# A retention layer with a SwiGLU feed-forward on one core: one pair's preparation and the end transposes earlier in the written order, and 29 stores issued by GpSimd

## The chip, the cores and the metric

The kernel runs on one core of a Trainium2 chip. The metric is the device time of one execution in microseconds; lower is better. A core has TensorE (PE; PEld is its loading of weights), VectorE (DVE), ScalarE (ACT), GpSimd (POOL) and SyncE (SP, which only issues transfers here). They run on their own and meet at semaphores. Transfers can be issued by SP, ACT and POOL; all of them are carried out by the same 16 DMA engines.

## The reference

```python
# q, k, v: 8 x 8 heads x 576 x 64, float32
scores = q @ k.transpose(0, 1, 3, 2) / sqrt(64)
gamma = 1 - 2 ** (-5 - arange(8))                  # one per head
Dmat = where(i >= j, gamma ** (i - j), 0)          # i: query, j: key
attn = (scores * Dmat) @ v                         # no softmax
x = attn.transpose(0, 2, 1, 3).reshape(4608, 512)
g = x @ w_gate                                     # 512 x 1536, float64 as given
out = (g * sigmoid(g) * (x @ w_val)) @ w_out       # 1536 x 512; out is 4608 x 512, float32
```

## The kernel before, in words

The attention is done in chunks of 64 tokens, for 32 pairs of heads (8 batches, 4 pairs each). Because the decay is a power of gamma, each chunk needs only its own scores, and a 64 x 64 state that carries all earlier chunks. The work on a pair is a pipeline of `tick(t)`: pair t is prepared (`transposes`: ScalarE multiplies the keys by powers of gamma at line 531, VectorE transposes q and k at line 516), pair t-1 gets its states (TensorE, line 567) and scores (line 597), and pair t-2 gets its values (lines 556, 583), which go to the matrix x. The first four pairs leave out their last chunk. These four last chunks are done together: GpSimd loads them early (`end_loads`, lines 711 and 716), VectorE transposes them (`end_transposes`, line 721), and TensorE makes their scores at line 727 (`end_scores`), as part of tick 6.

The weights are given as 64-bit floats. They are loaded in 18 blocks (lines 394 and 396), each block in two halves, and each half is turned to 32-bit: `split(j)` on ScalarE (lines 413, 414) takes the bits apart, and `rounding(j)` on VectorE (lines 430, 431) puts them together again. `rounding(j)` also writes `split(j + 1)` into ScalarE's order. A block's place in SBUF is reused, so a split also releases the load of a later block.

The feed-forward is done in tiles of tokens. The first tile (512 tokens) uses the weights as they are: `up0(f)` for 12 groups of features (TensorE into two of four PSUM banks, ScalarE's Silu at line 880, VectorE's product at line 881), then `down0(f)` (line 888). The later four tiles of 1024 tokens replace 32 block products by 26: the tables `UP`, `DOWN` and `OUT_SUMS` say which sums of blocks are multiplied. The sums of weights are made once. Those of w_gate and w_val are made by GpSimd during the first large tile (`w_sums`, through `add` at line 910, and line 1078) and sent to DRAM. Those of w_out are made earlier, during the first tile, for each third (`qd`) of the 1536 rows: GpSimd makes thirds 0 and 1, VectorE third 2 (`out_sums`, through `add`, lines 903 to 910). Each third has 26 sums of 128 x 256, made in 9 groups; a sum goes into a free place (six for GpSimd at first, six more from the last up0 on), is stored in DRAM by a transfer at line 961 that SP issues, and its place is free when that transfer has landed and no later sum reads it. A few of the 26 are a block itself, and need no sum.

The order is written out by hand: the schedule is manual, and each engine does its instructions in the order in which the program emits them. The list `plan` (lines 1217 to 1247) emits the roundings, `up0`, the ticks, the loads of later pairs and the first ten groups of sums. After it comes the loop over `down0` with the rest of the groups. SP's queue is in order too: it holds loads of q, k and v (lines 306, 311) and the stores of line 961, and a transfer whose condition isn't met holds those behind it.

Of the kernel before, what the change touches and what calls it, by code (L numbers as in the profile page):

```python
# [155 lines left out]
def kernel(  # L156
# [32 lines left out]
    nc = tc.nc  # L189
# [5 lines left out]
    HP = H // 2  # L195
# [7 lines left out]
    TB = TW // 4  # L203
# [63 lines left out]
    def whole(i):  # L267

        return HP <= i < needed(2) - 2
# [194 lines left out]
    def light(i):  # L464

        return needed(1) - 6 <= i < needed(2) - 2
# [119 lines left out]
    def scores(i, alone):  # L586

        qT = st[i]["qT"]
        for hl in range(0 if i < HP else 2):
            at = ts(NC - 1, L)  # L590
            nc.tensor.matmul(sr[half[hl]], kT[half[hl], at], qT[half[hl], at],  # L591
                             start=alone, stop=True, skip_group_check=True)
        for c in range(NFULL):
            for hl in range(2):
                for r in range(2):
                    at = ts(2 * c + r, L)
                    nc.tensor.matmul(sc[chunk(i, hl, 2 * c + r)[0], r if whole(i) else hl, c], kT[half[hl], at], qT[half[hl], at],  # L597
                                     start=True, stop=True, skip_group_check=True)
# [162 lines left out]
    def tick(t, lo=HP, hi=NP, spread=False, then=None):  # L761
        go_on(len(pieces))
        if hi == HP:

            def new_pair():
                scores(t - 1, True)
                new_states(t - 1)
                pieces.extend(masked(t - 1))
                go_on(3)

            scale_run(t + 1)
            if lo < t < hi:
                new_pair()
            if lo <= t - 2 < hi:
                own_values(t - 2)
            for f in transposes(t) if lo <= t < hi and t + 1 < HP else ():
                f()
            if lo <= t - 2 < hi:
                earlier_values(t - 2)
                if t == HP:  # L780
                    up0(0, range(2))
                to_x(t - 2)[0]()
            if t + 1 == HP:
                split(0)
                after = transposes(t)
                rounding(0)
                for f in after:
                    f()
            if t == HP:
                rounding(2)  # L790
                rounding(3, False)
                new_pair()
                while held:
                    held.pop()()
                split(4)
                up0(1, range(2))
            return
        if lo <= t - 2 < hi:
            own_values(t - 2)
            if t == HP + 3:  # L800
                st[t - 2]["own"] = end_own(1)
        if lo <= t - 1 < hi:
            new_states(t - 1)
        if lo <= t - 2 < hi:
            earlier_values(t - 2)
            if t == HP + 3:
                end_own(0)
                end_earlier()
        if lo <= t - 1 < hi:
            scores(t - 1, t - 2 < lo)  # L810
            if t == HP + 2:
                end_scores()
        if lo <= t - 1 < hi and whole(t - 2) and not whole(t - 1):
            decay(slice(0, H), slice(0, H), half[1])
        copies, *masks = masked(t - 1) if lo <= t - 1 < hi else (lambda: None,)
        keys, *new = transposes(t) if lo <= t < hi else (lambda: None,)
        outputs = to_x(t - 2)[0] if lo <= t - 2 < hi else lambda: None
        late = needed(1) - 4 <= t < needed(1) - 2 or light(t - 2)
        if late and masks:
            own, (last, pairs, odd, evens) = masks  # L820
            pieces.extend([lambda: (copies(), own(), last(), outputs()), [pairs, odd, lambda: (evens(), keys())]])
        elif late:
            pieces.append(lambda: (copies(), outputs(), keys()))
        else:
            pieces.extend([lambda: (copies(), keys()), outputs])
            for own, (last, pairs, *rest_of) in [masks] if masks else []:
                pieces.extend([own, [lambda: (last(), pairs()), *rest_of]])
        if then and new:
            pieces.extend(new[:-1])
            pieces.append(lambda: (new[-1](), then()))  # L830
        else:
            pieces.extend(new)
            pieces.extend([then] if then else [])
        if t == HP + 2:
            pieces.append(end_masks)
        if t == HP + 3:
            pieces.append(end_to_x)
        if not spread:
            go_on(len(pieces))
# [8 lines left out]
    def go_on(n):  # L848
        for _ in range(min(n, len(pieces))):
            while part_on():  # L850
                pass
# [61 lines left out]
    dn_ops = [dr.tile([P, 768], F32, name=f"dn{i}") for i in range(N)]  # L913
# [5 lines left out]
    x0_places = [rest[:, x0_at + TB * i : x0_at + TB * (i + 1)] for i in range(8)]  # L919
    vector_places = x0_places + more_places[6:] + [rest[:, part_at + TB * i : part_at + TB * (i + 1)] for i in range(8)]  # L920

    events = []
    for line in OUT_SUMS:
        i, s = line.split("|")
        slot, ops = s.split(":")
        events += [(int(op[1]), op) for op in terms(ops)] + [(None, int(slot), int(i))]

    def out_sums(qd):


        place = {}

        def free(p):
            if not any(p is q for q in x0_places):
                sum_places.append(p)

        eng, sum_places = (nc.vector, vector_places) if qd + 1 == NQ else (nc.gpsimd, pool_places)

        def view(s):
            return w_dn[:, qd, s // 2, s % 2] if s < 8 else place[s]  # L940

        def used(e):
            return [e[1]] if e[0] is None else [int(a) for a in e[1][2:]]

        def release(k):

            for s in list(place):
                for e in events[k + 1 :]:
                    if s in used(e):
                        break  # L950
                    if s == e[0]:
                        free(place.pop(s))
                        break
                else:
                    free(place.pop(s))

        def do(k):
            e = events[k]
            if e[0] is None:
                _, slot, i = e  # L960
                nc.sync.dma_start(out=dn_ops[i][:, qd * TB : (qd + 1) * TB], in_=view(slot))
            else:
                new = sum_places.pop(0)
                add(eng, e[1], view, new)
                if e[0] in place:
                    free(place[e[0]])
                place[e[0]] = new
            release(k)

        r, ends = [], [k for k, e in enumerate(events) if e[0] is None]  # L970
        for g in range(0, N, 3):
            lo, hi = ends[g - 1] + 1 if g else 0, ends[min(g + 2, N - 1)] + 1

            def group(lo=lo, hi=hi):
                for k in range(lo, hi):
                    do(k)

            r.append(group)
        return r
# [228 lines left out]
    FIRST = needed(1) - 2  # L1208
# [8 lines left out]
    plan = []  # L1217

    def round_until(i):
        while todo and order.index(i) >= todo[0]:  # L1220
            m = todo.pop(0)
            plan.extend(lambda j=j: rounding(j) for j in (2 * m, 2 * m + 1))

    round_until(3)
    tick_at = {2: 4, 3: 5, 5: 6, 7: 7, 10: 8, 11: 9}
    for f in range(2, NF):
        round_until({4: 12, 6: 13, 8: 14, 9: 15, 10: 16, 11: 17}.get(f, f + 2))
        if f == 2:
            plan.append(lambda: tick(HP, HP, FIRST))
        plan.append(lambda f=f: up0(f, range(HP)))  # L1230
        if f - 1 in tick_at and f < 7:
            plan.append(lambda t=tick_at[f - 1]: next_load(t))
        if f in tick_at and f > 2:
            if tick_at[f] == HP + 2:
                plan.append(end_transposes)
            plan.append(lambda t=tick_at[f]: tick(t, HP, FIRST))
        if f in (7, 10, 11):
            plan.append(lambda t=tick_at[f]: next_load(t))
        for _ in range({7: 3, 10: 4, 11: 3}.get(f, 0)):
            if f >= (7, 10, NF)[groups[0][0]]:  # L1240
                if f + 1 == NF and more_places:
                    plan.append(lambda places=more_places[:6]: pool_places.extend(places))
                    more_places.clear()
                plan.append(lambda group=groups.pop(0)[1]: group())
    assert not todo
    for f in plan:
        f()
    tick_at = {1: 10, 3: 11, 6: 12, 8: 13}
    for m, f in enumerate(down_order):
        down0(f)  # L1250
# [77 lines left out]
```

## Time and profile before

| | us |
|---|---|
| median of 3 runs (lowest, highest) | 1043.01 (1038.88, 1045.0) |
| the profiled execution | 1040.52 |
| its span, first to last instruction | 1038.8 |
| TensorE busy in it | 1022.6 |
| VectorE busy | 634.5 |
| GpSimd busy | 428.7 |
| ScalarE busy | 298.3 |

The page of a profile gives the busy time of each engine, then the span in 40 slices of 26 us: each digit is the busy share of a slice in tenths. Further views give the waits (engine, line, what it waited for: total us, times, longest), and the timeline (start in us, duration in us, engine, line, operation, tiles written <- read, shapes, count; in brackets the idle time before it and what ended that). "SPq" and "ACTq" are transfers being issued. A line in the profile can be that of a helper: line 910 is an addition from `add`, whoever called it.

### The profile page before, as it was taken

To read this page: it belongs to the slowest core of one execution; us is meant where nothing else is said; L and a number is where in the kernel's file an instruction comes from. 1 tells how busy PE (TensorE), PEld (TensorE's weight loads), DVE (VectorE), ACT (ScalarE), POOL (GpSimd) and SP (SyncE) were. 2 spreads that over 40 slices of the span, in tenths; PEclk is the share of its full clock that TensorE was granted. 3 is DMA by queue.
4 is the path that set the end of the run, shared out by engine and by line. 5 is a ranking of instruction groups with operands and counts; after the bars stand their busy time and mean duration, and the time that the engine had idled before them with its cause. 6 is when DMAs were issued, how large, how long until landed. Compare 5 with 4: busy or idle time off the path is not lost.

```text
span 1038.8 us, 21564 instructions
## 1 busy us (share of the span) xinstructions
PE 1022.6 (98%) x8440; PEld 846.2 (81%) x8440; DVE 634.5 (61%) x1070; ACT 298.3 (29%) x649; POOL 428.7 (41%) x377
## 2 busy tenths in 40 slices
PE   6999999999999999999999999999999999999998
PEld 5644555888888888888888888888888888888887
DVE  5388878776758767546457685435466644344644
ACT  4375523243534222222322103223211022231110
POOL 3402367776575236622134058212242583222425
PEclk9999999999999999999999999999999999999999
DMA  9999877776779887674686687545554465555553
GB/s 245 249 279 257 198 208 268 210 206 192 192 201 245 227 249 217 179 198 140 187 223 178 177 201 218 152 138 153 154 174 149 145 197 150 155 153 161 180 163 100
DMA packets 307244, 199.12 MB, mean 192 GB/s; under 512 B 215944, under 2 KB 251784, under 8 KB 307144
## 3 DMA queue, kind: packets, MB, share of 16 engines
q1 hardware_dynamic: 275720, 161.17, 57.9%
q10 hardware_dynamic: 30784, 36.18, 10.5%
q8 instruction: 67, 1.10, 0.5%
q0 software_dynamic: 640, 0.39, 0.2%
q14 instruction: 33, 0.27, 0.1%
HBM read 157.58 MB, written 40.11 MB: 190 GB/s over the span
## 4 chain that ended last, share of the span: by engine, by line
PE 73%; DVE 0%; POOL 0%; ACT 0%; ACTq 0%; issue 0%; DVEq 0%
PE bankC L1107 11%; PE bankE L1107 11%; PE bankB L1107 11%; PE bankA L1107 11%; PE bankC L1156 7%; PE bankB L1156 7%; PE bankE L1156 7%; PE bankA L1156 7%; PE outer L556 1%; PE outer L583 1%; PE inner L597 1%; PE inner L567 1%; PE outer L591 0%; PE outer L579 0%; DVE arena L1134 0%; POOL arena L1078 0%
## 5 line engine op out<-in xcount | busy, mean ns | idle before, releaser
L1044 POOL TENSOR_TENSOR rest<-rest 128x512 f32<-128x512 f32 x65 | 91.6, 1414 | 234.7 <-DVE rest L1044 213.7
L1128 ACT ACTIVATE io<-rest 128x256 f32<-128x256 f32 x180 | 75.0, 416 | 302.5 <-DVE rest L1044 260.2
L1107 PE MATMUL bankC<-rest,arena 128*128 128x256 f32 x544 | 129.2, 381 | 0.0
L1107 PE MATMUL bankA<-rest,arena 128*128 128x256 f32 x544 | 128.8, 380 | 0.0
L910 POOL TENSOR_TENSOR arena<-arena 128x512 f32<-128x512 f32 (+1 forms) x72 | 110.8, 1551 | 35.8 <-DMA up<-arena 20.3
L1107 PE MATMUL bankE<-rest,arena 128*128 128x256 f32 x512 | 121.4, 380 | 1.0 <-DVE rest L1044 1.0
L1107 PE MATMUL bankB<-rest,arena 128*128 128x256 f32 x512 | 121.3, 380 | 0.2 <-DVE rest L1044 0.2
L1135 POOL TENSOR_TENSOR arena<-rest,io 128x256 f32<-128x256 f32 x72 | 51.9, 726 | 167.8 <-ACT io L1128 167.8
L1107 PEld LDWEIGHTS bankA<-rest,arena 128*128 128x128 f32 x544 | 103.3, 190 | 14.5 <-issue 0.7
L1107 PEld LDWEIGHTS bankC<-rest,arena 128*128 128x128 f32 x544 | 103.0, 190 | 14.4 <-POOL arena L910 0.3
L1107 PEld LDWEIGHTS bankE<-rest,arena 128*128 128x128 f32 x512 | 97.1, 190 | 14.5 <-DVE rest L1044 1.4
L1107 PEld LDWEIGHTS bankB<-rest,arena 128*128 128x128 f32 x512 | 97.2, 190 | 13.6 <-issue 0.6
L910 POOL TENSOR_TENSOR rest<-rest 128x256 f32<-128x256 f32 (+1 forms) x66 | 67.7, 1046 | 77.3 <-DVE rest L431 38.4
L1044 DVE TENSOR_TENSOR rest<-bankB,rest 128x512 f32<-128x512 f32 x72 | 48.9, 687 | 66.0 <-PE bankB L1107 51.7
L1044 DVE TENSOR_TENSOR rest<-bankC,rest 128x512 f32<-128x512 f32 x72 | 48.9, 688 | 65.7 <-PE bankC L1107 44.0
L1044 DVE TENSOR_TENSOR rest<-bankA,rest 128x512 f32<-128x512 f32 x72 | 48.9, 687 | 60.6 <-PE bankA L1107 44.1
L1044 DVE TENSOR_TENSOR rest<-bankE,rest 128x512 f32<-128x512 f32 x71 | 48.2, 688 | 59.6 <-PE bankE L1107 46.7
L1131 DVE SCALAR_TENSOR_TENSOR arena<-rest,io 128x256 f32<-128x256 f32 x84 | 58.6, 698 | 10.9 <-ACT io L1128 10.9
L1156 PE MATMUL bankB<-arena 128*128 128x256 f32 x252 | 58.2, 381 | 0.0
L1156 PE MATMUL bankC<-arena 128*128 128x256 f32 x252 | 58.2, 381 | 0.0
L1156 PE MATMUL bankE<-arena 128*128 128x256 f32 x252 | 57.9, 380 | 0.0
L1156 PE MATMUL bankA<-arena 128*128 128x256 f32 x252 | 57.9, 380 | 0.0
(205 smaller groups left out, 1632.3 us busy)
## 6 DMA issues: line engine op xcount, KB each, us to landing
arena<-up SPq DMA_DIRECT2D x234, 256.0 KB, 2.7
arena<-dn SPq DMA_DIRECT2D x104, 384.0 KB, 3.9
up<-arena ACTq DMA_DIRECT2D x78, 256.0 KB, 4.1
dn<-rest SPq DMA_DIRECT2D x78, 128.0 KB, 1.8
out_dram<-rest SPq DMA_DIRECT2D x31, 256.0 KB, 3.9
qk<-in_q_dram SPq DMA_DIRECT2D x108, 72.0 KB, 2.6
qk<-in_k_dram SPq DMA_DIRECT2D x108, 72.0 KB, 3.0
rest<-in_moe_w_out_dram ACTq DMA_DIRECT2D x6, 1024.0 KB, 5.7
```

Source lines behind the costliest of these rows:

```text
L556: m = nc.tensor.matmul(value(i, hl, c), s["v"][rows, at], ret[rows, c % 2 if whole(i) else hl, c // 2], start=start, stop=start, skip_grou ...
L567: nc.tensor.matmul(z[half[hl], r, c], s["kn"][chunk(i, hl, 2 * c + r)], s["v"][rows, at], start=True, stop=True, skip_group_check=True)
L583: nc.tensor.matmul(xr[half[hl]] if c + 1 == NC else value(i, hl, c), state[half[hl], c, :], s["qT"][half[hl], ts(c, L)], start=False, stop ...
L597: nc.tensor.matmul(sc[chunk(i, hl, 2 * c + r)[0], r if whole(i) else hl, c], kT[half[hl], at], qT[half[hl], at], start=True, stop=True, sk ...
L910: eng.tensor_tensor(out=dst, in0=srcs[0], in1=srcs[1], op=ALU.add if op[0] == "add" else ALU.subtract)
L1044: eng.tensor_tensor(out=at(op[1]), in0=at(op[2]), in1=at(op[3]), op=ALU.add if op[0] == "add" else ALU.subtract)
L1107: m = nc.tensor.matmul(b[:, gv * TB : (gv + 1) * TB], w[:, gv, ts(c, P)], rhs[:, c, :], start=(opens and gv == 0 and c == 0), stop=(c == 1 ...
L1128: nc.scalar.activation(out=s, in_=src[:, 0:TB], func=AF.Silu, scale=-1.0 if negative else 1.0)
L1131: return lambda: nc.vector.scalar_tensor_tensor(out=dst, in0=src[:, TB : 2 * TB], scalar=-1.0, in1=s, op0=ALU.mult, op1=ALU.mult)
L1135: nc.gpsimd.tensor_tensor(out=dst, in0=src[:, TB : 2 * TB], in1=s, op=ALU.mult)
L1156: nc.tensor.matmul(b[:, m * TB : (m + 1) * TB], lhs[:, qd, ts(m, P)], w[:, qd], start=(opens and qd == 0 and m == 0), stop=(qd == NQ - 1), ...
```

## The change

Three edits. The preparation of pair 4 (`tick(HP, HP, FIRST)`, which is only `transposes(4)`) was emitted after four roundings, just before `up0(2)`; now it is emitted after the first of them. The end transposes were emitted before tick 6; now they are emitted after tick 5. And a store of a sum that GpSimd made is issued by GpSimd itself as long as the plan is being emitted: these are the 26 stores of third 0 and the first three of third 1. The order of TensorE's instructions is the same as before; so is the order of the loads in SP's and ScalarE's queues.

```diff
+    down_begun = []
...
             if e[0] is None:
                 _, slot, i = e
-                nc.sync.dma_start(out=dn_ops[i][:, qd * TB : (qd + 1) * TB], in_=view(slot))
+                queue = nc.gpsimd if eng is nc.gpsimd and not down_begun else nc.sync
+                queue.dma_start(out=dn_ops[i][:, qd * TB : (qd + 1) * TB], in_=view(slot))
...
     round_until(3)
+    plan.insert(1, lambda: tick(HP, HP, FIRST))
     tick_at = {2: 4, 3: 5, 5: 6, 7: 7, 10: 8, 11: 9}
     for f in range(2, NF):
         round_until({4: 12, 6: 13, 8: 14, 9: 15, 10: 16, 11: 17}.get(f, f + 2))
-        if f == 2:
-            plan.append(lambda: tick(HP, HP, FIRST))
         plan.append(lambda f=f: up0(f, range(HP)))
...
         if f in tick_at and f > 2:
-            if tick_at[f] == HP + 2:
+            plan.append(lambda t=tick_at[f]: tick(t, HP, FIRST))
+            if tick_at[f] == HP + 1:
                 plan.append(end_transposes)
-            plan.append(lambda t=tick_at[f]: tick(t, HP, FIRST))
...
     for f in plan:
         f()
+    down_begun.append(True)
```

## The prediction

> **What bounds the kernel now.** I read the page first: the share of each engine, then the slices.
>
> ```profile
> PE 1022.6 (98%) x8440; PEld 846.2 (81%) x8440; DVE 634.5 (61%) x1070; ACT 298.3 (29%) x649; POOL 428.7 (41%) x377
> DMA  9999877776779887674686687545554465555553
> ```
>
> TensorE is busy for 98% of the span, so 1038.8 - 1022.6 = 16.2 us of waits is all that an edit of order can win. The DMA engines are full in the first four slices (to 104 us), which matters for anything that is stored earlier. Next, what TensorE waits for between 50 and 200 us, the stretch that the diff touches:
>
> ```profile
> PE inner L567 <- ACT kn L531: 1.2, 1, 1.2
> PE outer L727 <- DVE rest L721: 1.2, 1, 1.2
> PE bankE L1107 <- DVE rest L1044: 1.0, 1, 1.0
> PE bankB L1107 <- DVE rest L1044: 0.2, 1, 0.2
> ```
>
> Four waits, 3.6 us in all; outside them TensorE runs without a gap. The timeline places the first two:
>
> ```profile
> 50.91 0.66 ACT L413 ACTIVATE rest<-rest 128x512 f32<-128x512 f32 x1 [9.58 <-DMA rest<-in_moe_w_gate_dram]
> 54.85 0.96 ACT L531 ACTIVATE kn<-kn,tab 128x256 f32<-128x256 f32 x2
> 55.41 1.08 PE L567 MATMUL inner<-v,kn 64*64 64x64 f32 x29 [1.20 <-ACT kn L531]
> 73.65 0.76 DVE L721 STREAM_TRANSPOSE rest<-rest 128x256 f32<-128x256 f32 x2
> 74.47 0.46 PE L727 MATMUL outer<-rest 64*64 64x64 f32 x16 [1.16 <-DVE rest L721]
> ```
>
> ScalarE stood idle for 9.58 us until a weight block landed, and then did three splits before the keys of pair 4 (L531). VectorE reached the end transposes (L721) only after the product of up0(5). The third view is the queues and GpSimd:
>
> ```profile
> 119.18 6.11 POOL L910 TENSOR_TENSOR rest<-rest 128x256 f32<-128x256 f32 x7 [28.55 <-DMA dn<-rest]
> 137.59 0.72 POOL L910 TENSOR_TENSOR rest<-rest 128x256 f32<-128x256 f32 x1 [9.30 <-DMA dn<-rest]
> 168.34 3.38 POOL L910 TENSOR_TENSOR arena<-arena 128x512 f32<-128x512 f32 x2
> ```
>
> ```profile
> 114.22 9.41 SPq L961 DMA_DIRECT2D dn<-rest x9
> 123.73 3.42 SPq L306 DMA_DIRECT2D qk<-in_q_dram x4
> 131.35 45.42 SPq L961 DMA_DIRECT2D dn<-rest x69
> ```
>
> GpSimd has six places for sums. Their stores stand in SP's queue behind the loads of q, k and v, so GpSimd waits 28.6 and then 9.3 us, does its last 36 instructions for w_out from 137.6 to 168.3 us, and goes straight into the sums of the up weights, which TensorE reads from 176.3 us on. That it waited cost TensorE nothing there; what it does is to put GpSimd's sums beside VectorE's sums of x, and the last stores (176.3 us) ahead of them (VectorE waits 2.3 us for stores). The two waits of 1.27 us at 188 and 192 us are VectorE being late from this.
>
> **What the Trainium skill says.** "DMA: Bandwidth & Descriptors", section "Issuing engines are not separate DMA queues": the issuing engine saves only issue time, the transfers share 16 engines. This fits the full DMA row above. "SBUF — State Buffer", section "Who interferes with whom": a VectorE instruction with two SBUF inputs, or in a two-port mode, excludes GpSimd's reads and the other way round, while matrices read from PSUM don't. The trace agrees: a rounding (L430 and L431) takes 0.42 + 0.69 us alone, 0.94 + 1.10 at 120.6 us beside a sum; L604, which reads PSUM, keeps 0.69. The same page warns that software-made descriptors starve beside VectorE's two-port modes. The trace shows little of it: the twenty loads that GpSimd issued at 30 to 46 us took 548 to 763 ns each (128 pieces, as many as a store has), and the roundings beside them kept 0.42 and 0.69 us.
>
> **The change part by part.** TensorE's order is the same; SP loses 29 stores (26 of the first third of w_out, 3 of the second), GpSimd gains them; VectorE and ScalarE each have a group moved.
>
> *Keys and transposes of pair 4* now stand after one rounding instead of after four. Their k was issued at 38.7 us; loads near there took 7.1 to 7.9 us, so it is there at about 46.5, and the q and k for the transposes at 45.6. VectorE waits there (it idled from 43.4 to 51.6 us anyway); the transposes (0.77 + 0.74 us) end at 47.1 and the rounding behind them at 48.2, before TensorE needs it at 50.6. The keys (0.96 us) end at about 47.5, inside ScalarE's 9.58 us of idleness. Gain 1.20 us. What is late next is bank A: ScalarE read it at 55.70, after the keys; without them that is 54.85 to 55.45, and TensorE wants it at 57.05 - 1.20 = 55.85. It just fits.
>
> *The end transposes* move ahead of the roundings at 64.4 us. Their loads (issued to 46 us, 4.0 to 6.8 us to landing) are there. They cost VectorE 0.76 us, and the transposes and the product before them come earlier by about as much. Gain 1.16 us. So TensorE is ahead by 2.36 us at 75 us.
>
> *The stores on GpSimd.* Each costs it some 0.6 us of issue (548 to 763 ns above). The first third is 27 instructions at 0.855 us (30.8 us for the 36 above) and 26 stores: 23.1 + 15.6 = 38.7 us from about 83 us, to 122. The second is 23.1 + 3 x 0.6, to 147 us if nothing holds it. Before, it was 168.3. So there are 168.3 - 147 = 21 us of room, 0.8 us a store, for landings. About four places are in flight; if each store takes 6 to 7 us to land while the DMA engines are full (the small ones took 4.0 to 6.8 there), the pace is about 1.9 us a store and the first third ends near 132, the whole near 157. SP's load of pair 10, at 123.7 us behind nine stores, comes some 3 us sooner, and 29 x 0.4 us of issue leave its queue. VectorE then finds its places free and GpSimd quiet at 165 to 180 us. I take the full 1.27 us; at worst nothing of it.
>
> *What that costs.* Ten roundings (95 to 112 us) had GpSimd idle beside them (91 to 119 us) and now have it busy with sums some 60% of the time. Beside back-to-back sums a rounding lost 0.42 us (84 to 90 us) to 0.89 us (120 to 124 us): 10 x 0.6 x 0.42..0.89 = 2.5 to 5.3 us. The cover is this:
>
> ```profile
> 112.75 0.68 ACT L413 ACTIVATE rest<-rest 128x512 f32<-128x512 f32 x1 [2.73 <-DMA rest<-in_moe_w_out_dram]
> 114.51 0.69 DVE L881 TENSOR_TENSOR arena<-bankB,io 128x512 f32<-128x512 f32 x1 [2.67 <-PE outer L591]
> 124.63 0.68 DVE L881 TENSOR_TENSOR arena<-bankE,io 128x512 f32<-128x512 f32 x1
> 126.89 1.02 PE L888 MATMUL bankE<-rest,arena 128*128 128x512 f32 x2
> ```
>
> VectorE idles 2.67 us at 112 us (really behind ScalarE, which waits for the last w_out block), and bank E is free 126.89 - 125.31 = 1.58 us before it is needed: 4.25 us of cover, enough for most of the range. The last block of w_out (issued at 104.4, landed at 112.7) is the other way in: 12 to 14 stores of 128 KB now travel between 85 and 112 us, 1.7 MB beside some 7 MB. A quarter more on 8.35 us is 2 us, and it is issued about 1 us later against TensorE; 3 us less the 1.58 leaves 1.4 us. The two overlap. Bounds are 0 and 3.5 us; I take 0.8.
>
> Sum: 1.20 + 1.16 + 1.27 - 0.8 = 2.8 us, with 3.6 and 0 as ends of the ordinary. On the profiled execution, 1040.5 us with a span of 1038.8, that gives 1037.7 and 1036.0. The median of the runs shown is 2.5 us above that execution, so on its scale I say 1040.2.
>
> **The rivals.**
>
> *The gain is given back.* VectorE late at bank E by the upper figure (3.5 us) and the waits at 188 us still there: 2.36 - 2.36..3.5 = 0 to -1.1, so 1043 to 1044. For it: the cover of 4.25 us is used on two sides, and the DMA row is at 9. Against: VectorE's own chain is released by TensorE, so it moves with it.
>
> *GpSimd becomes late: slower.* Sums wait for stores about four back. If a store lands in more than some 9 us (pace over 2.3 us over all 26), the 21 us of room are gone, the sums of the up weights start after 168 us, and TensorE waits at 178 us for them (their slack is 2.9 us now, less the 2.36 us it is ahead). At 12 us a landing while DMA is full, 7 stores are done by 112 us, and the rest at 1.8 us end at 146; plus 25 is 171, hardly late. At a pace of 2.8 us throughout, 26 x 0.5 = 13 us late less the gain of 2.4: 1053. For it: a full DMA row, and GpSimd stands still in each wait. Against: landings of 4.0 to 6.8 us there, 1.8 us for SP's stores later. That the other two moves fail is part of neither: TensorE's waits name them.
>
> *More than is visible*, 1036 or less: nothing but the 3.6 us in this stretch is on TensorE's path, so only chance.
>
> **How the numbers follow.** Forecast 0.58 (1038 to 1042), given back 0.22, GpSimd late 0.14, more 0.06. The three runs of before spread over 6 us, which widens each case by 2 us or so. 0.5%, 5.2 us, is about what a measurement of this kernel can tell from no change. Faster by more (under 1037.8): the rival "more" and the lower edge of the forecast, 0.16. Slower by more (over 1048.2): nearly all of GpSimd late, and a little of chance, 0.16. Range for 8 in 10: 1035.5 to 1048; the forecast's own is 1037.5 to 1042.5.
>
> **What would show it.** Right: no wait of L567 for L531 and none of L727 for L721; the keys at 46 to 48 us; GpSimd's sums from 83 us with stores between them of about 0.6 us, the first third done by 135 and all by 160 us; SP's first stores after 128 us; roundings at 95 to 112 us of 1.3 to 1.7 us; at most 1.5 us of waiting at down0's first bank E near 124.5 us; none at 188 us. Wrong: a wait of TensorE for a sum of GpSimd (L1078 or L910) after 174 us, stores on GpSimd over 1 us each, a wait of L888 over 2.4 us, or of up0 for a rounding between 90 and 115 us.

## The result, and the profile after

The change made the kernel a little slower: 1046.18 us median (1044.15 to 1051.35, 20 runs) against 1043.01 (1038.87 to 1049.23, 20 runs), a ratio of 1.0036 with a 95% interval of 1.0023 to 1.0050. The forecast was 1040.2. The profiled execution took 1045.22 us with a span of 1043.5; before, 1040.52 and 1038.8. That is 4.7 us of span to account for; the medians differ by 3.2, since the profiled execution of before lies 2.5 us below its median and that of the change 1.0 below. (Behind line 962 the lines have moved by two: L1107 is now L1109. Kernels that hold loads back have one more line early on: there L877 is L878.)

The rows of engines on the page, TensorE and GpSimd in the first line, and the row of the DMA engines:

```profile
PE 1022.9 (98%) x8440; PEld 846.4 (81%) x8440; DVE 639.5 (61%) x1070; ACT 299.1 (29%) x649; POOL 442.1 (42%) x406
DMA  9999875677688987664676677555554565555553
```

TensorE has the same work (1022.6 before), so nearly all of it is waits. GpSimd has 29 instructions more, the issues, and 13.4 us more of busy time; VectorE is busy for 5.0 us more with the same 1070 instructions.

The waits of TensorE between 50 and 200 us (engine, tile and line, what it waited for, total, times, longest):

```profile
PE bankA L877 <- ACT io L880: 3.2, 2, 2.8
PE inner L567 <- issue: 1.6, 1, 1.6
PE outer L591 <- DVE kT L516: 1.2, 1, 1.2
PE outer L556 <- DVE ret_last L614: 0.8, 1, 0.8
PE bankE L888 <- DVE arena L881: 0.8, 1, 0.8
```

None of the four waits of before is left: L567 for ScalarE's keys, L727 for the end transposes, and the two of L1107 are all gone. In their place stand 7.6 us of others, and the timeline of TensorE places them:

```profile
105.98 3.70 PE L877 MATMUL bankA<-rest,arena 128*128 128x512 f32 x8 [2.79 <-ACT io L880]
123.47 0.46 PE L556 MATMUL outer<-ret,v 64*64 64x64 f32 x16 [0.82 <-DVE ret_last L614]
125.50 0.69 PE L567 MATMUL inner<-v,kn 64*64 64x64 f32 x32 [1.57 <-issue]
131.16 1.12 PE L888 MATMUL bankE<-rest,arena 128*128 128x512 f32 x2 [0.79 <-DVE arena L881]
148.51 0.28 PE L591 MATMUL outer<-qT,kT 64*64 64x64 f32 x2 [1.15 <-DVE kT L516]
```

TensorE's order is the same in both kernels, so the start of one matmul can be set against the start of the same matmul before. Read so from the two timelines:

| TensorE's instruction | before, at us | after, at us | later by | step |
|---|---|---|---|---|
| up0(6) on bank B, L877 | 78.40 | 75.75 | -2.65 | the two moves |
| the last before up0(10), bank E, L877 | 102.24 | 99.59 | -2.65 | |
| up0(10) on bank A, L877 | 105.67 | 105.98 | +0.31 | +2.96 |
| down0 on bank B, L888 | 125.17 | 128.49 | +3.32 | +3.01 |
| down0 on bank E, L888 | 126.89 | 131.16 | +4.27 | +0.95 |
| down0 on bank B after pair 10's values | 143.82 | 150.20 | +6.38 | +2.11 |
| the up product on bank E, L1107 and L1109 | 191.80 | 196.52 | +4.72 | -1.66 |

The moves brought their 2.65 us, the waits at 188 and 192 us gave back 1.66, and four steps cost 9.03 us between them. The last row is the difference of the spans. The first three of those steps come from one place, VectorE's roundings between 96 and 121 us. The windows view of L430 and then of L431 over this stretch, first of before, then of after (window, length, VectorE's busy time and number, granted clock, DMA share, GB/s):

```profile
95.00:120.65 25.65, 4.23 (x11) 1.00 0.92 235
95.00:120.65 25.65, 6.93 (x10) 1.00 0.92 235
```

```profile
95.00:120.65 25.65, 10.23 (x10) 1.00 1.04 289
95.00:120.65 25.65, 11.91 (x10) 1.00 1.04 289
```

The ten roundings took 11.1 us before (the eleventh instruction only begins here) and take 22.1 after. The timelines of VectorE and of GpSimd show how:

```profile
97.29 1.74 DVE L431 CUSTOM_DVE_ANT_0 arena<-arena,rest 128x1024 uint16<-128x1024 uint16 x1
98.95 1.42 DVE L430 TENSOR_SCALAR arena<-rest 128x512 int32<-128x512 int32 x1
```

```profile
96.11 0.74 POOL L910 TENSOR_TENSOR rest<-rest 128x256 f32<-128x256 f32 x1
97.14 0.56 POOL L963 DMA_DIRECT2D dn<-rest  x1 [0.30 <-POOL rest L910]
97.73 0.74 POOL L910 TENSOR_TENSOR rest<-rest 128x256 f32<-128x256 f32 x1
98.76 0.56 POOL L963 DMA_DIRECT2D dn<-rest  x1 [0.30 <-POOL rest L910]
99.34 1.62 POOL L910 TENSOR_TENSOR rest<-rest 128x256 f32<-128x256 f32 x2
```

A store is issued in 0.56 us, 0.30 us after the sum that it sends, and the next sum follows at once. VectorE's instruction of 97.29 us came during the store of 97.14. It ended at 99.03, 0.56 us after the sum behind that store (97.73 + 0.74 = 98.47), which is nearly all of its own 0.69 us. The next one, of 98.95, came during the next store and ended behind the first of the two sums that follow it. So 0.69 became 1.74 and 0.42 became 1.42. Nine of the twenty instructions are of this kind, 1.33 us or more, and all nine came 0.13 us or more after the start of a store that had a sum ready behind it. Two others came within 0.03 us of the start of such a store and took 1.07 and 0.69 us. Two came during a store with a second store behind it, and they took their own time, 0.42 and 0.41 us. One of these two, and the next instruction, which came during the second store and met the sum of 108.27 us:

```profile
107.11 1.15 POOL L963 DMA_DIRECT2D dn<-rest  x2 [0.30 <-POOL rest L908]
107.57 0.42 DVE L430 TENSOR_SCALAR arena<-rest 128x512 int32<-128x512 int32 x1
108.02 1.55 DVE L431 CUSTOM_DVE_ANT_0 arena<-arena,rest 128x1024 uint16<-128x1024 uint16 x1
```

ScalarE takes turns with VectorE over the weights, and so it comes late to bank A:

```profile
97.28 0.68 ACT L413 ACTIVATE rest<-rest 128x512 f32<-128x512 f32 x1 [2.90 <-DVE arena L430]
104.78 0.66 ACT L414 ACTIVATE rest<-rest 128x512 int32<-128x512 uint32 x1 [1.20 <-DVE rest L431]
105.34 0.59 ACT L880 ACTIVATE io<-bankA 128x512 f32<-128x512 f32 x1
```

Its splits wait for roundings, the Silu that reads bank A (L880) stands behind them, and up0(10) needs that bank: 2.79 us. At 122 us VectorE is still late. It does the attention of pair 9 behind the roundings; its last step there (L632) frees `inner`, and L567 starts 0.11 us after it, which explains the wait that the profile puts down to "issue":

```profile
124.92 0.47 DVE L632 SCALAR_TENSOR_TENSOR state<-state,tab,inner 128x256 f32<-128x256 f32 x1
```

The fourth step, at 148 us, is another thing. ScalarE issues the loads of pair 11, and its next copy (L608) stands behind them in its order. Its timeline before:

```profile
128.62 2.48 ACTq L306 DMA_DIRECT2D rest<-in_k_dram  x4
132.60 0.39 ACTq L311 DMA_DIRECT2D kn<-in_k_dram  x1
135.08 0.39 ACTq L311 DMA_DIRECT2D v<-in_v_dram  x1
135.59 0.37 ACT L608 COPY even<-inner 128x256 f32<-128x256 f32 x1 [9.04 <-DMA rest<-in_k_dram]
```

And after:

```profile
132.67 6.36 ACTq L306 DMA_DIRECT2D rest<-in_k_dram  x4
140.68 0.39 ACTq L311 DMA_DIRECT2D kn<-in_k_dram  x1
141.61 0.39 ACTq L311 DMA_DIRECT2D v<-in_v_dram  x1
142.12 0.37 ACT L608 COPY even<-inner 128x256 f32<-128x256 f32 x1 [12.02 <-DMA dn<-rest]
```

The issues begin 4 us later and take longer, so L608 is 6.5 us late, VectorE's transposes of pair 10 with it, and TensorE loses 2.11 us more. The four issues of k are not slow in themselves (0.32 to 0.63 us each). The first two are over at 133.9 us, and then ScalarE stands until the third:

```profile
138.12 0.32 ACTq L306 DMA_DIRECT2D rest<-in_k_dram  x1
```

By the semaphores in the trace this issue waits for the landing of pair 10's keys, which SP had issued at 132.69 us; they are there at 138.10. It is so in all nine kernels of this document that take the 29 stores out of SP's queue, one of which issues no early store at all, and in none of the five that leave them there. So the longer stretch is not the early stores' traffic: with those stores out of SP's queue, later issues wait for other transfers than before. Why they do is not shown by any run.

### The profile page after: what moved, and what is told of

It reads as the page before. It is cut to its first block, busy times and chain, and to the rows that moved or that the text cites. A ratio compares the mean times of both kernels' runs of the same rounds, so it can differ in the third digit from the quotient of the medians.

```text
span 1043.5 us, 21555 instructions
## 1 busy us (share of the span) xinstructions
PE 1022.9 (98%) x8440; PEld 846.4 (81%) x8440; DVE 639.5 (61%) x1070; ACT 299.1 (29%) x649; POOL 442.1 (42%) x406
## 4 chain that ended last, share of the span: by engine, by line
PE 73%; DVE 0%; POOL 0%; ACT 0%; ACTq 0%; issue 0%; DVEq 0%
PE bankC L1109 11%; PE bankE L1109 11%; PE bankB L1109 11%; PE bankA L1109 11%; PE bankB L1158 7%; PE bankC L1158 7%; PE bankE L1158 6%; PE bankA L1158 6%; PE outer L556 1%; PE inner L597 1%; PE outer L583 1%; PE inner L567 1%; PE outer L591 0%; PE outer L579 0%; DVE arena L1136 0%; POOL arena L1080 0%
## 5 line engine op out<-in xcount | busy, mean ns | idle before, releaser
L1109 PE MATMUL bankC<-rest,arena 128*128 128x256 f32 x544 | 129.1, 380 | 0.0
L1109 PE MATMUL bankA<-rest,arena 128*128 128x256 f32 x544 | 128.7, 380 | 0.0
L1109 PE MATMUL bankE<-rest,arena 128*128 128x256 f32 x512 | 121.3, 380 | 0.0
L1109 PE MATMUL bankB<-rest,arena 128*128 128x256 f32 x512 | 121.2, 380 | 0.0
L1109 PEld LDWEIGHTS bankA<-rest,arena 128*128 128x128 f32 x544 | 103.4, 190 | 14.3 <-issue 0.5
L1109 PEld LDWEIGHTS bankC<-rest,arena 128*128 128x128 f32 x544 | 103.0, 190 | 14.4 <-POOL arena L910 0.3
L1109 PEld LDWEIGHTS bankB<-rest,arena 128*128 128x128 f32 x512 | 97.3, 190 | 13.1
L1109 PEld LDWEIGHTS bankE<-rest,arena 128*128 128x128 f32 x512 | 97.2, 190 | 13.1
L1133 DVE SCALAR_TENSOR_TENSOR arena<-rest,io 128x256 f32<-128x256 f32 x84 | 59.0, 704 | 10.9 <-ACT io L1130 10.4
```

The costliest lines, as they stand in the source:

```text
L1109: m = nc.tensor.matmul(b[:, gv * TB : (gv + 1) * TB], w[:, gv, ts(c, P)], rhs[:, c, :], start=(opens and gv == 0 and c == 0), stop=(c == 1 ...
L1133: return lambda: nc.vector.scalar_tensor_tensor(out=dst, in0=src[:, TB : 2 * TB], scalar=-1.0, in1=s, op0=ALU.mult, op1=ALU.mult)
```

## The experiments

### The two moves alone

All stores go back to SP.

```diff
-                queue = nc.gpsimd if eng is nc.gpsimd and not down_begun else nc.sync
+                queue = nc.sync
```

> The two moves alone; all 78 stores are issued by SyncE as before. Theory A (GpSimd's sums and stores hold up VectorE's roundings, 11.1 us for ten of them before, 21.5 us after) and theory B (the stores' traffic makes the weight blocks late) both say that the waits of L567 and L727 are gone and nothing new stands at 106 us: 1.2 + 1.16 us faster than before, ratio about 0.9977, less up to 1.9 us if the transposes of pair 11 (0.43 us of slack before) don't keep up. Ten roundings from 91 to 120 us take about 11 us. Theory C (the moves themselves bring the loss, by blocking VectorE and ScalarE behind the loads of pair 4) says slower than before.

Measured: 1044.9 us (1041.5 to 1047.46, 14 runs) beside 1043.78 of the kernel before, a ratio of 1.0007 (0.9990 to 1.0023). The ten roundings are back at 11.1 us. TensorE is 1.85 us ahead at up0(10) and 0.58 us behind at the first up product, near 175 us. The waits of TensorE from 50 to 200 us:

```profile
PE outer L591 <- DVE kT L516: 1.8, 1, 1.8
PE bankC L1109 <- POOL arena L1080: 1.3, 1, 1.3
PE bankA L877 <- ACT io L880: 0.8, 1, 0.8
```

What follows: the moves take away both waits and win nothing that can be measured. ScalarE issues the v of pair 11 at 135.13 us, against 135.08 before, and does L608 behind it at 135.64: the issue of v waits in both for the last of the k loads, which lands at 135.06 us before and at 135.11 here, and doesn't follow TensorE. A TensorE that comes 1.85 us earlier waits 1.83 us there. There is a smaller sign of the same kind: SP issues the k of a later pair at 88.07 us, against 84.37 before, and ScalarE stands 2.04 us for it, which TensorE does not feel yet.

### The stores alone

Only the store's edit; the preparation of pair 4 and the end transposes stay where they were.

> The stores on GpSimd alone, without the two moves. A and B: the loss is all here, 4 to 6 us slower than before, ratio 1.004 to 1.006; A says that ten roundings take 20 us or more and TensorE waits some 0.5 to 3 us for ScalarE at bank A of up0(10), with the weight blocks no later than TensorE's delay. C: the same as before within 1 us.

Measured: 1047.57 us (1044.78 to 1050.43, 22 runs), a ratio of 1.0034 (1.0023 to 1.0044). The roundings are stretched as in the change, and TensorE waits 0.72 us at bank A of up0(10), 0.83 and 1.57 at pair 9, 0.78 at bank E and 1.34 for kT. The profile also has a wait of 3.01 us for pair 4's keys at 57 us (1.20 before), ahead of all GpSimd stores. What follows: the stores alone cost as much as the whole change (1.0034 beside 1.0036), just under the 1.004 that both theories named as the least.

### Sums without stores, and stores without sums

In the first, the 29 stores are left out where they stood, and other values are written at the end of SP's queue; in the second, GpSimd's sums of third 0 are left out and 26 stores remain. Neither computes all of w_out's sums, and only the stretch to 130 us is to be compared.

```diff
-                queue.dma_start(out=dn_ops[i][:, qd * TB : (qd + 1) * TB], in_=view(slot))
+                if eng is nc.gpsimd and not down_begun:
+                    later.append((i, qd))
+                else:
+                    nc.sync.dma_start(...)
```

```diff
-                add(eng, e[1], view, new)
+                if qd:
+                    add(eng, e[1], view, new)
```

> The changed kernel, but the 29 early stores are left out; SyncE writes 29 blocks of w_out in their places after the first tile, so the output is not the reference's. GpSimd's sums then run without stores between them, from about 84 to 112 us. If the sums alone hold up VectorE: a rounding beside them takes 1.8 to 2.2 us. If it is the pair of a store and a sum that holds the shared access: a rounding beside sums alone takes 1.5 to 2.0 us, against 2.15 with stores between. B says that the roundings don't matter, and that with the early traffic gone the wait at bank A of up0(10) is gone whatever they take.

> The changed kernel, but the sums of the first third are left out: GpSimd issues its 26 stores one after the other, of blocks of w_out, from about 84 us, so the output is not the reference's. If issuing a store holds up VectorE by itself: the roundings from 84 to 100 us take 1.6 us or more. If only sums do (alone or behind a store): they keep 1.11 us each. B says that the traffic, now denser (3.4 MB in some 16 us), makes a weight block late and TensorE waits over 2 us between 90 and 125 us.

Measured: with sums alone the ten roundings take 16.1 us in all, between 1.11 and 2.02 each, and up0(10) waits 0.61 us at bank A. With stores alone eight of the ten take 1.11 to 1.16 each, as before; the other two (1.41 and 1.73) stand beside sums of the next third, which begin at 112.17 us. The 26 stores are all issued by 102.9 us, so only four of the twenty instructions fall beside one; with those from 84 us on there are nine, and each kept 0.42 to 0.47 or 0.69 us. A pair of VectorE instructions beside back-to-back sums, and one with stores all around it (GpSimd issued three in 1.74 us from 101.19 us on):

```profile
98.04 1.10 DVE L431 CUSTOM_DVE_ANT_0 arena<-arena,rest 128x1024 uint16<-128x1024 uint16 x1
99.06 0.95 DVE L430 TENSOR_SCALAR arena<-rest 128x512 int32<-128x512 int32 x1
```

```profile
101.75 0.43 DVE L430 TENSOR_SCALAR arena<-rest 128x512 int32<-128x512 int32 x1 [2.50 <-ACT rest L413]
102.32 0.69 DVE L431 CUSTOM_DVE_ANT_0 arena<-arena,rest 128x1024 uint16<-128x1024 uint16 x1
```

What follows: in this run a store by itself doesn't hold VectorE up; a sum costs a rounding about half a microsecond (5.0 us over the ten); both in turn cost 11.0. So the excess belongs to the pair. The second kernel shows another thing beside it: with stores packed this densely the k of a pair, issued at 89.27 us, is there 10.9 us later (5.2 in the change), ScalarE stands 8.93 us for it, and bank A of up0(10) waits 3.36 us. Theory B expected such a wait, for a weight block. That the dense stores make this load late is likely but not shown: with no early store at all it took 7.4 us. Harm of the same size can come this way, and had to be told apart.

### The traffic taken away

The changed kernel, with 16 of 256 columns in each early store.

```diff
+                if eng is nc.gpsimd and not down_begun:
+                    nc.gpsimd.dma_start(out=dn_ops[i][:, qd * TB : qd * TB + 16], in_=view(slot)[:, 0:16])
+                    later.append((i, qd))
```

> The changed kernel, but each of GpSimd's 29 early stores carries 16 of its 256 columns (8 KB for 128 KB); the whole places are filled by SP at the very end with other values, so these sums of w_out are not what the kernel needs. GpSimd's instructions and their order stay, 94% of the early stores' bytes go. Theory A (instructions: a store with a sum behind it keeps VectorE out): the ten roundings keep 20 to 22 us in sum, and up0(10) keeps a wait at bank A of over 1.5 us. Theory B (traffic): the roundings fall to 16 us and the wait to under 0.7 us. What comes after 180 us is not to be compared.

Measured: the ten roundings take 19.2 us, and bank A waits 3.06 us. What follows: with 94% of the bytes gone, most of the excess stays; it is GpSimd's instructions and not their traffic. The verdict is less clean than it was meant to be. The 19.2 lies a little below the 20 that was named for this reading. And part of the wait has another source: the k of a pair landed 7.5 us after its issue here, as late as with sums and no stores (7.4), so the bytes of the stores are not the cause, and ScalarE began its splits late. The stretch that isn't touched by this, from the first split behind those keys that waits for VectorE or an issue to the Silu of bank A, holds three splits: 4.3 us before, 8.1 in the change, 7.0 here, and 5.2 in the kernel with grouped stores, which follows.

### Stores in groups

The same stores, each group's issued by GpSimd after the group's last sum.

```diff
+                if queue is nc.gpsimd:
+                    at_end.append(lambda: queue.dma_start(out=out, in_=src))
...
                 for k in range(lo, hi):
-                    do(k)
+                    do(k, at_end)
+                for store in at_end:
+                    store()
```

> The changed kernel, but GpSimd issues the stores of a group of sums together, after the last sum of that group, so that about one sum in three stands directly behind a store instead of nearly every one. Theory A (a VectorE instruction that arrives during a store waits until the end of the sum behind it): the ten roundings of 91 to 120 us fall from 21.5 us to 16 to 17.5 us (the kernel with these sums and no stores had 16.1), the wait of up0(10) at bank A (2.8 us) falls under 1 us, and the time is 1.5 to 3 us under that of the change, 0.9985 to 1.002 of the kernel before. Theory B (the traffic of the stores, 26 x 128 KB, is what makes the last weight blocks and so the roundings late): the bytes are the same and go out a little more bunched, so the roundings keep 20 us or more in sum, up0(10) waits 2 us or more, and the ratio stays at 1.003 to 1.005.

Measured: 1045.71 us (1043.69 to 1049.68, 17 runs), a ratio of 1.0020 (1.0007 to 1.0033), 1.7 us less than the change by the ratios, though the two intervals overlap. The ten roundings take 15.5 us, and bank A waits 0.18 us. TensorE is still 1.4 us ahead at down0's bank B. What follows: the same bytes and the same instructions in another order give 6.6 us of VectorE's time back. Not all of it is the order of store and sum. With its stores issued late, GpSimd stands for free places (3.80 us at 105.8, 1.18 and 0.83 us elsewhere), and three of the ten roundings fall into its longest pause, with no sum beside them. One instruction was held amid three stores (1.22 us for 0.69 at 112.53), which no theory here explains. The waits that remain, of L556 for ScalarE's L650 (2.12 us) and of L591 for kT (1.04 us) between 141 and 146 us, lie behind pair 11's loads. From bank E at 126 us to 174 us TensorE loses 6.8 us, 3.2 in these waits and 3.4 by its clock (last section), which takes back what grouping had won.

### Something else behind the store

The changed kernel, with a memset of 128 x 1 behind each early store.

> The changed kernel, and behind each of GpSimd's 29 early stores a memset of one column of a scratch tile, so that the instruction standing behind a store is no longer a sum. Theory A1 (it is the sum waiting behind the store that already holds the port while the store is issued): a VectorE instruction gets in between store and sum; the long forms of 1.42 and 1.74 us go, the ten roundings fall from 21.5 to 17 us or less, and bank A of up0(10) waits under 1.2 us. Theory A2 (the store itself holds the port, or the sum alone does and the store only lines VectorE up with it): the long forms stay, the sum of the ten is 20 us or more, and the time is that of the change or up to 2 us over it.

Measured: 1045.39 us (1041.33 to 1050.13, 20 runs), a ratio of 1.0026 (1.0012 to 1.0041). GpSimd in it, the VectorE instruction that came during this store, and the next, which came 0.13 us into the store of 107.16 us:

```profile
105.50 0.56 POOL L964 DMA_DIRECT2D dn<-rest  x1 [0.30 <-POOL rest L910]
106.06 0.12 POOL L966 MEMSET spacer<- 128x1 f32 x1
106.12 0.74 POOL L910 TENSOR_TENSOR rest<-rest 128x256 f32<-128x256 f32 x1
105.67 1.48 DVE L430 TENSOR_SCALAR rest<-rest 128x512 int32<-128x512 int32 x1
107.29 0.69 DVE L431 CUSTOM_DVE_ANT_0 rest<-rest 128x1024 uint16<-128x1024 uint16 x1
```

The ten roundings take 17.4 us, near the 17 that theory A1 named and well under the 20 of A2, though GpSimd has more to do; three of the twenty instructions are still of the long form (1.38, 1.48 and 1.70 us). Bank A waits 0.68 us. Eight instructions came during a store with a memset and a sum behind it. Three of them came 0.12 to 0.14 us after its start and took 0.69 us; in the change the three that came at that time took 1.74. What follows: what stands behind the store decides, and not the store alone. But the memset lets in only those that come this early: the five that came 0.17 us or later were held past the sum all the same (1.11 to 1.70 us). (This run's profile also has a wait of 4.5 us at 59.8 us, ahead of all GpSimd stores, which is not the edit's.)

### Pair 11's loads held back

The k and v of pair 11 are issued by ScalarE after the pieces of tick 10, once with the moves alone and once with the full change.

```diff
+                    go = lambda queue=queue, dst=dst, src=src: queue.dma_start(...)
+                    held_loads.append(go) if i == needed(1) - 3 else go()
...
             tick(tick_at[m], HP, FIRST, tick_at[m] + 1 < needed(1))
             go_on(2)
+            while held_loads:
+                held_loads.pop(0)()
```

> The two moves alone (all stores on SP), and the loads of k and v of pair 11, which ScalarE issues at 135.1 us and which hold its copies for pair 10 behind them, are emitted after the pieces of tick 10. Theory C (the 2.36 us won by the moves are lost again mainly at pair 11's keys, a wait of 1.83 us at L591 near 142.7 us, because these loads are released at a fixed time): that wait goes, TensorE is still about 2 us ahead at the first L1109, and the ratio to the kernel before is 0.9975 to 0.999, against 1.0007 for the moves alone. Rival (the moves' gain is lost to VectorE and to the sums of x after 160 us whatever stands at 142 us): the wait goes, others appear at L1109 or L1158, and the ratio stays within 0.9995 to 1.001.

> The changed kernel with the loads of k and v of pair 11, which ScalarE issues between 132 and 142 us, emitted after the pieces of tick 10. Theory D (2.1 us of what the change loses, between 131 and 149 us, is ScalarE standing in the issue of these loads, which come later and go slower than before because GpSimd's stores travel beside them): the wait of L591 for kT near 148.5 us goes, TensorE is 1.5 to 2.1 us less late at the first up product, and the median is 1 to 2 us under that of the change, 1.0015 to 1.003 of the kernel before. Rival (those 2.1 us are VectorE, late from the roundings): the wait stays, with another releaser, and the ratio too.

Measured: with the moves alone 1043.56 us (22 runs) beside 1044.06, a ratio of 1.0000 (0.9988 to 1.0013); with the full change 1043.64 us (22 runs) beside 1041.99, a ratio of 1.0015 (1.0000 to 1.0030). In both the wait of L591 for kT is gone. With the full change TensorE's lag is 5.02 us at down0's bank B and 4.61 at 188 us, so the 2.11 us of the fourth step are not lost. What follows: that step is these loads. The four issues of k still take long (6.85 us), but ScalarE's copy no longer waits for the k and v behind them, and starts at 139.58 us instead of 142.12. With the moves alone the lead does reach the first up product (2.16 us at 178 us), and is then given away in one go:

```profile
PE bankA L1110 <- POOL arena L911: 1.7, 1, 1.7
PE bankE L1110 <- DVE rest L1047: 1.0, 1, 1.0
PE bankB L1110 <- DVE rest L1047: 0.9, 1, 0.9
```

GpSimd's sums of the up weights, which follow the last of w_out, come at their old time, and VectorE's sums of x with them. This was the rival of that run, and it held there.

### A version that beats both

The held loads, and one more edit: up0(2) stands ahead of rounding 9, so that its Silu isn't behind split 10 in ScalarE's order, which made up0(4) wait 0.43 to 0.85 us at bank A. First with all stores on SP, and then with GpSimd's stores in groups.

```diff
-        plan.append(lambda f=f: up0(f, range(HP)))
+        if f == 2:
+            plan.insert(len(plan) - 1, lambda f=f: up0(f, range(HP)))
+        else:
+            plan.append(lambda f=f: up0(f, range(HP)))
```

> As the run with pair 11's k and v held, and up0(2) is emitted ahead of rounding 9, so that ScalarE's Silu of up0(2) does not stand behind split 10; that was the 0.8 us wait of up0(4) at bank A near 56.6 us. Theory C: this wait goes as well, 0.4 to 0.8 us more are kept, ratio 0.997 to 0.9985, the fastest of all so far. Rival: rounding 9 comes later by one product, and split 10 with it; then up0(4) waits for its weights instead, and the ratio is no better than that of the run before.

> The fixed moves once more (both moves, up0(2) ahead of rounding 9, pair 11's k and v held, all stores on SP), for a narrower interval and beside the last run on one chip: 0.9975 to 0.9995 of the kernel before if TensorE's 2.7 us at 240 us last to the end; 0.9995 to 1.001 if the first run's 0.9993 is what is left of them.

> All that the runs so far point to: both moves, up0(2) ahead of rounding 9, pair 11's k and v held, and GpSimd's early stores issued by GpSimd but together after the sums of a group. Theory: TensorE is 2.7 to 3.1 us ahead at 100 us as in the run with the fixed moves, loses 1.5 to 2.5 us to the roundings and to bank E by 130 us, no more at 145 us, and wins the 1.3 us at 188 us that the fixed moves alone do not: ratio 0.997 to 0.999. Rival (any store on GpSimd in this stretch costs as much as it wins): 0.9995 to 1.002, behind the fixed moves alone.

Measured: with stores on SP 1042.09 us (14 runs) beside 1044.06, a ratio of 0.9993 (0.9976 to 1.0010), and again 1041.77 us (22 runs) beside 1041.99, a ratio of 0.9988 (0.9976 to 1.0001). With grouped stores 1037.99 us (1036.68 to 1039.84, 7 runs) beside 1041.99, a ratio of 0.9947 (0.9924 to 0.9969). Its waits from 50 to 200 us:

```profile
PE bankA L878 <- ACT io L881: 1.1, 1, 1.1
PE inner L568 <- issue: 0.7, 1, 0.7
PE bankE L889 <- DVE arena L882: 0.5, 1, 0.5
```

What follows: the roundings (15.1 us), and keys that landed 8.8 us after their issue, still cost 2.3 us of waits, but nothing is lost at pair 11, and nothing for VectorE's sums at 188 us, where the version with stores on SP waits 0.9 and 1.0 us in its two profiles. The stores on GpSimd are worth having, as far as seven runs tell, once they are issued together and ScalarE isn't tied to the loads. In the profile this version is 1.1 us ahead of the kernel before at 250 us and its span is 0.8 us less, while the medians differ by 4.0 us. The profiled executions are not typical: this one, 1039.72 us, is 1.7 us above its median, and that of before 1.5 us below the 1041.99. The profiles account for 0.8 us; where the rest of the 4 us is won isn't shown. It is not the granted clock: of the 60 runs of before beside it, the 30 at a mean clock of 1.000 have a median of 1041.88 us.

## Why the prediction was wrong

The range held the time, 1046.18 in 1035.5 to 1048; the likeliest case and its sign were wrong, and the rival "the gain is given back" stopped short at 1044.

- *Keys and transposes of pair 4, end transposes, 2.36 us.* Right as a step: 2.65 us ahead from 75 to 102 us. "It just fits" at bank A did not quite hold: 0.43 us of wait in the change, 0.85 with the moves alone. But as an addend to the sum it failed. The run with the moves alone shows that the kernel doesn't carry it to the end: pair 11's loads come at a time that doesn't follow TensorE, and so, in three of the four runs with the moves and stores on SP, do GpSimd's sums of the up weights (waits of 1.3, 1.7 and 0.3 us). The prediction asked what is late next at 56 us and nowhere after.
- *GpSimd's timing.* Right: issues of 0.56 us in the median (0.6 was taken), the first third done by 127 us (by 135), all sums by 155.3 us (by 157 to 160). Landings were quicker than assumed, 4.1 us in the median and 6.5 at most (6 to 7 was taken). GpSimd was never what TensorE waited for, so the rival "GpSimd becomes late" fell.
- *The 1.27 us at 188 and 192 us.* Right in size: 1.66 us came back there. For the change this is partly luck, since TensorE came there 6 us late, and its waits would have gone with no help from GpSimd. The reason given is borne out by the fastest version: TensorE came 0.67 us late and waited for nothing, where some 0.6 us of the 1.27 would otherwise have remained.
- *SP's load of pair 10, some 3 us sooner.* Wrong: at 126.81 us against 123.73. The stores no longer stood ahead of it, but its place did: VectorE's transposes of pair 9 end at 126.74 us and free it. The queue was one of two conditions, and the other was late.
- *What that costs, 0.8 us.* This is the step that failed; it was 9.0 us. Three faults lie in it. The size: "10 x 0.6 x 0.42..0.89 = 2.5 to 5.3 us" counted GpSimd as in the way only while it sums and took its issues as harmless, from loads that no sum stood behind. It was 11.0 us. The run with sums alone gives 5.0, inside that estimate, and the run with stores alone gives nothing; the pair of a store and a sum ready behind it, which neither row of before shows, makes the rest. The cover: "4.25 us" counted what lies at 112 and 124 us, while the first to be late was at 105 us, by ScalarE's splits and bank A. The last: the loads of pair 11 (2.11 us), which the prediction doesn't name. They are late because VectorE is, and one of their issues waits for pair 10's keys, which it didn't before.
- Of the signs named, the wait of up0 for roundings between 90 and 115 us came, through ScalarE. A wait of L888 over 2.4 us did not: other waits ahead of it took the delay.

## What to carry to other kernels

Before a DMA issue is moved onto an engine that computes, ask what stands behind it there: the cost may be neither the issue nor the computation, but the two taken as one. A gap closed early in a kernel is won only if nothing downstream keeps its own time: list the transfers and engines that don't follow the bound engine, and fix the first of them along with the move. Taking transfers out of a queue can also change which earlier transfers the later issues wait for: look at every issue behind them again. And a cover is counted at every place where the delayed engine is waited for, through the engines that take turns with it, not at the place where it last idled.

## What the runs showed of the hardware

*The port between VectorE and GpSimd.* The Trainium skill's "SBUF — State Buffer", section "Who interferes with whom", says that the pair of ports is an exclusive lock for a whole instruction, held by whoever issues first. The traces agree and add to it: with a sum ready behind a store, a VectorE instruction that came 0.13 us or more after the store's start stood for the rest of the store and all of the sum, 1.33 to 1.74 us for 0.42 to 0.69, nine times of nine in the change; one that came within 0.03 us of the start, or with a second store behind, was not held so; with a memset of 0.12 us between, those at 0.12 to 0.14 us got in and those from 0.17 us on did not. Each that was held in the change ended 0.29 us (L430) or 0.56 us (L431) after the end of the sum. That the lock is taken when the sum is handed on, shortly after the issue of the store begins, is the reading that fits these; the lock itself isn't in any trace, and two instructions amid grouped stores (1.22 us for 0.69, and 0.95 for 0.42 in the fastest version) don't fit it. The page also warns of stores starved by VectorE: little of that is seen in the change, where they took 0.54 to 0.71 us each.

*A short wait can cost a second time.* In seven of the fourteen traces TensorE's granted clock falls for a while, each time while it stood still or within 2 us after. In the full change with held loads it waited 1.92 and 1.57 us up to 125.9 us. A window around the end of these waits, and then the stretch of the low clock alone (window, length, busy time and instructions of TensorE, weight loads, VectorE, ScalarE and GpSimd, then the clock, DMA share, GB/s):

```profile
125.00:130.00 5.00, 4.08 (x122) 3.76 (x123) 4.79 (x9) 0.31 (x2) 4.91 (x8) 0.66 0.68 174
125.40:128.81 3.41, 2.89 (x103) 2.92 (x107) 3.38 (x6) 0.00 (x0) 3.39 (x6) 0.50 0.62 196
```

The clock is halved for 3.41 us. In the window of 5 us the lost clock is 0.34 x 5 = 1.7 us, as it is after a wait of 2.26 us with the fixed moves (0.66 in one window), after one of 3.01 us with the stores alone (0.88 and 0.77) and after one of 3.06 us with the small stores (0.86 and 0.80); with grouped stores it is 3.4 (0.86, 0.50 and 0.96). "TensorE: Matmul & The Clock Gate", "Part 1: The HAM clock gate", has the clock at half after an idle window of about 3.4 us. The halved stretch is as long as that window; but waits of 2.1 and 2.3 us were enough for it here, while the 2.79 us of the change's own profile and the 3.36 us of the run with stores and no sums brought none. Over an execution 1.7 us is 0.0016 of the clock. The mean clock was 0.9988 over the 140 runs of the kernel before that stood beside the experiments, of which 61 were at 1.000; 0.9978 over 20 of the change, of which 5 were; and 1.000 in all 7 of the fastest version. From this some 0.001 x 1043 = 1 us of the change's loss would be not waiting but the clock after it. That is an estimate: the 5 runs of the change at 1.000 have a median of 1045.22 us, 1.0 us below that of all 20, but the runs of before at 1.000 are faster than all by 1.4 us in one set of 45 and by 0.1 us or not at all in the two others.
